# Two top-k chains in turn on VectorE, and one pool of float32 buffers for x, the result and the MLP's activations

## The chip, the cores and the metric

The kernel runs on one core of one Trainium2 chip. The metric is the device time of one execution in microseconds. The kernel before was run three times: 1166.22, 1166.27 and 1168.5 us, median 1166.27. A profiler recorded one more execution; its rows are shown further below.

## The reference

The inputs are q, k and v of shape 4 x 8 x 576 x 64 (batch, heads, sequence, head size, float32) and the weights of two MLPs, each 512 x 2048 and 2048 x 512, which come as float64. The output is 2304 x 512 float32.

```python
scores = scale * np.matmul(q, k.transpose(0, 1, 3, 2))          # 576 x 576 for each of 32 heads
kth = np.partition(scores, -32, axis=-1)[..., -32:-31]
scores = np.where(scores >= kth, scores, -1e9)                  # the 32 largest of each row stay
attn = softmax(scores); x = attn @ v                            # 2304 tokens x 512 (heads side by side)
h = np.maximum(x @ w_in, 0.0);  x = h * h @ w_out               # first MLP
h = x @ w2_in;  x = (h * np.clip(h + 3, 0, 6) / 6) @ w2_out     # second MLP
```

## The kernel before, in words

**Numbers.** Every matrix is scaled by a power of two and split into two float16 parts, a high and a low one; a product is three float16 matmuls (high x high, high x low, low x high). The float64 weights are turned to float32 by integer operations on VectorE (lines 363 and 366), completed by an addition on GpSimd (line 413), bounded by a Gram matmul (line 429) and split through TensorE and ScalarE (lines 537 to 546), for the last matrix through ScalarE and GpSimd.

**Attention.** The 576 query rows of a batch are four blocks of 128 and one of 64; a block has a tile for each head, in the block of 64 rows one for each pair of heads. That makes 20 blocks and 144 tiles. A tile goes through these steps, each a task on one engine (function `attend`):

- TensorE multiplies q and k into PSUM (`qk`, line 768); ScalarE evacuates the scores to a float32 buffer S (line 774). There are three S buffers.
- VectorE finds the 32 largest of each row in seven large steps: the eight largest of S (line 782); then three times: replace the eight found (line 787, from S into W the first time, later W in place) and take the eight largest of W (line 790). In the kernel before there is one W buffer.
- VectorE scales the 32nd largest (line 799, "the threshold"), ScalarE makes a Relu of the distance to it (line 804, tile E), GpSimd subtracts that from S (line 807, "the mask"; it frees S), ScalarE takes the exponential (line 812).
- ScalarE and GpSimd split the result (lines 818 and 822), a DMA transposes it, TensorE multiplies by v (line 841).

**Between attention and MLP.** For each block `x_operand` copies the normalised product from PSUM to the float32 tile x (line 913), takes its norm (lines 922 and 926), scales x in place (line 933), and splits it (line 936 on ScalarE, line 939 on GpSimd). Then x is free.

**The MLPs.** The two blocks of 64 rows of neighbouring batches are joined, so there are 18 units of 128 rows. Each MLP is four groups per unit, 144 groups in all: 48 up-projection matmuls (line 1083) into one of two PSUM banks h, on ScalarE a Relu into a float32 tile r (line 1090 in the first MLP, line 1092 in the second), a square on ScalarE (line 1095) or a gate on VectorE (line 1098), the split (line 1105 on ScalarE, line 1108 on GpSimd; it frees r), and 12 output matmuls (line 1115) into `acc`. A unit's result is scaled from PSUM into the float32 tile o on ScalarE (line 1187) and stored by a DMA.

**What sets the order.** All steps are tasks of a planner that runs while the program is built. It simulates the five engines with given costs; whenever an engine is free it takes, of the tasks whose inputs and buffers are there, the one with the lowest key, offset + slope x position from the table `PRIO`. A buffer pool is a list of free slots, taken at a task's start and given back when the last user is done. The planner writes out one fixed order for each engine, and on the chip each engine works through its own in that order, waiting on semaphores. In the kernel before, pool `f` has two buffers and serves r alone; pool `x` has one and serves x and o.

Of the kernel before, what the change touches and what calls it, by code (L numbers as in the profile page):

```python
# [9 lines left out]
F32 = mybir.dt.float32  # L10
# [9 lines left out]
P = 128  # L20
# [12 lines left out]
class Plan:  # L33
# [7 lines left out]
    def pool(self, **sizes):  # L41
        for name, n in sizes.items():
            self.pools[name] = list(range(n))
# [21 lines left out]
    def free(self, name, owner, *users):  # L65
        e = [len(users), name, owner]
        for u in users:
            u.rel.append(e)
# [66 lines left out]
def tile_topk_attention_moe_moe2(  # L135
# [12 lines left out]
    B, H, S, D = q.shape  # L148
# [37 lines left out]
    task, free = plan.task, plan.free  # L186
    size, ncol = {}, [0]

    def pool(name, n, shape, dtype, where=None):

        plan.pool(**{name: n})
        size[name] = (shape, dtype, where or sb)
# [7 lines left out]
    def take(name, label=None):  # L200
        if name == "stg":
            return stg[plan.current.slot[name]]
        if isinstance(size[name], int):
            c = size[name] + plan.current.slot.get(name, 0)
            return scalars[:, c:c + 1]
        shape, dtype, where = size[name]
        return where.tile(shape, dtype, tag=f"{name}{plan.current.slot[name]}", name=label or name, bufs=1)
# [5 lines left out]
    acc_t = ps.tile([P, 2, 512], F32, name="acc")  # L213
    plan.pool(acc0=1, acc1=1)
    pool("S", SBUFS, [P, S], F32)
    pool("W", 1, [P, S], F32)
    pool("E", 2, [P, S], F32)
    pool("wc", 2, [P, 2 * S], F16)
    pool("wT", WTB, [P, 2 * S // P, P], F16)
# [3 lines left out]
    pool("vv", 4, [P, 2, 2, NCH, D], F16)  # L223
    plan.pool(stg=2)
    pool("qf", 1, [P, 4, D], F32)
    pool("x", XBUFS, [P, H, D], F32)
    pool("f", FBUFS, [P, 512], F32)
    pool("hl", HBUFS, [P, 2, KD, P], F16)
    pool("ghl", GBUFS, [P, 2, 512], F16)
# [653 lines left out]
    def x_operand(i):  # L883
# [3 lines left out]
        u = unit[i]  # L887
        o = off[i]
        tail = j == NFULL
        ntl = NHP if tail else H  # L890
        box = {}
# [11 lines left out]
                                        op0=ALU.mult, op1=ALU.mult)  # L903

        def copy():
            box["x"] = x = take("x")
            if o == 0:
                T["hl", u] = take("hl")
            a_ = T["av", i]
            for t in range(ntl):  # L910
                for hh in range(2 if tail else 1):
                    rows = slice(hh * TAIL, hh * TAIL + TAIL) if tail else slice(0, P)
                    nc.scalar.activation(x[0:n, 2 * t + hh if tail else t, :], a_[rows, t * D:(t + 1) * D], AF.Copy,  # L913
                                         scale=box["rv"][rows, t:t + 1])
# [26 lines left out]
        def flip():  # L941
# [4 lines left out]
        t1 = task("DVE", 0.3, ("xinv", first[i]), inverse, deps=masks, alloc=["rv"])  # L946
        free("sums", masks[0], t1)
        t2 = task("POOL", 1.0, ("xscales", first[i]), scales, deps=[t1] + [vv_task[b, hp][1] for hp in range(NHP)])
        avs = [av_tasks[i, t] for t in range(ntl)]
        t3 = task("ACT", 1.6, ("xcopy", first[i]), copy, deps=[t2, *avs, hl_task.get(u)],  # L950
                  alloc=["x"] + (["hl"] if o == 0 else []))
        hl_task.setdefault(u, t3)
        free("rv", t1, t3)
        free("av", avs[0], t3)
# [6 lines left out]
        t8 = task("ACT", act(H * D) + 0.09, ("xevac", first[i]), scaled, deps=[t7])  # L961
        t9 = task("ACT", act(H * D), ("xhigh", first[i]), high, deps=[t8])
        t10 = task("POOL", gps(H * D), ("xlow", first[i]), low, deps=[t9])
        free("x", t3, t10)
        l_ = task("SP", 1.25, ("xflip", first[i]), flip, deps=[t10], lat=WLAT)
        free("xh", t5, l_)
        opd_task.setdefault((0, u), []).append(l_)
# [88 lines left out]
    pos = {}  # L1056
# [5 lines left out]
    acc_task, ca_task, up_tasks = {}, {}, {}  # L1062
# [110 lines left out]
    def second_layer(u):  # L1173
        n = usize[u]
        for g in range(KF // (4 if n == P else 2)):
            group(1, u, g)
        free("hl", hl_task[u], up_tasks[1, u])
        box = {}

        def scale():  # L1180
            box["oc"] = take("oc")
            nc.gpsimd.tensor_scalar(box["oc"], T["ca", u], wp["c4"][:, 0:1], 1.0, op0=ALU.mult, op1=ALU.mult)

        def evac(ch):
            rows = min(P, n - ch * P)
            box["o", ch] = take("x", "o").rearrange("p h d -> p (h d)")
            nc.scalar.activation(box["o", ch][0:rows], acc_t[0:rows, 1 if n == P else ch, :], AF.Copy,
                                 scale=box["oc"][0:rows])

        def store(ch):  # L1190
            for i in units[u]:
                if off[i] // P == ch:
                    b, j = order[i]
                    r0, o_ = b * S + j * P, off[i] - ch * P
                    nc.sync.dma_start(out[r0:r0 + nof[i], :], box["o", ch][o_:o_ + nof[i]])

        t1 = task("POOL", 0.25, ("oscale", pos[1, u, 0]), scale, deps=[ca_task[u], wchain[3]], alloc=["oc"])
        free("ca", ca_task[u], t1, up_tasks[1, u])
        evacs = []
        for ch in range(-(-n // P)):  # L1200
            t2 = task("ACT", 0.57, ("oevac", pos[1, u, 0]), lambda ch=ch: evac(ch), deps=[t1, acc_task[1, u, ch]], alloc=["x"])
            free("acc1" if n == P else f"acc{ch}", acc_task["first", 1, u], t2)
            t4 = task("SP", 0.7, ("store", pos[1, u, 0]), lambda ch=ch: store(ch), deps=[t2])
            free("x", t2, t4)
            evacs.append(t2)
        free("oc", t1, *evacs)

# [45 lines left out]
def first_of(order, b):  # L1253
# [8 lines left out]
XBUFS = 1  # L1262
# [18 lines left out]


PRIO = {
    "load0": (340.23, 0.014),
    "load1": (350.41, 0.164),
    "load2": (928.87, 0.102),
    "load3": (-360.56, 0.044),
    "conv0": (67.49, 0.032),
    "bits0": (-334.56, 0.363),
    "add0": (363.46, 0.095),  # L1290
    "gram0": (733.07, 0.252),
    "conv1": (-463.48, 6.177),
    "bits1": (-2000.78, 3.588),
    "add1": (755.49, 12.573),
    "gram1": (-359.57, 3.788),
    "conv2": (-82.75, 2.263),
    "bits2": (-74.87, 5.088),
    "add2": (-377.68, 0.472),
    "gram2": (-991.89, 0.269),
    "conv3": (-1.27, 0.102),  # L1300
    "bits3": (-226.43, 28.692),
    "add3": (-84.33, 84.284),
    "gram3": (-161.59, 0.926),
    "norm": (219.01, 13.853),
    "high0": (-1412.47, 0.238),
    "low0": (-24.71, 0.477),
    "scaled0": (120.91, 11.399),
    "rest0": (-103.76, 1.596),
    "high1": (14.57, 0.624),
    "low1": (127.85, 0.860),  # L1310
    "scaled1": (330.42, 0.525),
    "rest1": (-81.15, 22.480),
    "high2": (293.37, 0.024),
    "low2": (630.00, 0.444),
    "scaled2": (806.32, 3.448),
    "rest2": (215.58, 5.372),
    "high3": (626.80, 1.338),
    "low3": (626.39, 0.081),
    "scaled3": (-343.44, 0.430),
    "rest3": (697.07, 8.977),  # L1320
    "qsquare": (632.65, 7.129),
    "qtotal": (-1166.11, 0.296),
    "qscale": (-195.35, 1.307),
    "ksquare": (141.52, 0.440),
    "ktotal": (-181.14, 0.255),
    "kscale": (-641.06, 0.456),
    "vsquare": (-1289.92, 1.322),
    "vtotal": (-247.36, 0.604),
    "vscale": (-270.58, 0.132),
    "clear": (-377.61, 0.641),  # L1330
    "kload": (52.44, 1.333),
    "vload": (216.40, 1.003),
    "qload": (178.65, 0.151),
    "qhigh": (232.24, 1.506),
    "qlow": (352.49, 0.502),
    "khigh": (1105.20, 0.462),
    "klow": (-595.14, 0.742),
    "vhigh": (649.09, 0.140),
    "vlow": (296.69, 1.624),
    "kflip": (-92.81, 0.020),  # L1340
    "qscales": (-1577.85, 0.028),
    "qflip": (-1853.07, 8.317),
    "qk": (-107.90, 1.290),
    "evac": (-234.65, 0.662),
    "topk": (301.64, 0.948),
    "bias": (-1723.17, 0.048),
    "lowest": (299.95, 1.000),
    "below": (164.49, 1.525),
    "mask": (-161.55, 1.964),
    "expo": (58.25, 1.189),  # L1350
    "whigh": (667.72, 2.141),
    "wlow": (812.95, 0.224),
    "wflip": (-102.44, 0.805),
    "av": (609.90, 0.441),
    "xinv": (-211.49, 3.990),
    "xscales": (-221.33, 3.583),
    "xcopy": (-212.46, 0.097),
    "xflip": (335.99, 3.918),
    "xsquare": (23.27, 0.207),
    "xtotal": (-357.75, 0.055),  # L1360
    "xscale": (184.03, 11.039),
    "xevac": (-411.77, 1.057),
    "xhigh": (-2455.71, 0.319),
    "xlow": (355.78, 0.352),
    "common": (420.79, 5.138),
    "ysquare": (2109.22, 0.583),
    "ytotal": (-237.40, 1.777),
    "yflip": (-429.37, 0.932),
    "yscale": (262.86, 0.157),
    "yhigh": (-121.73, 0.079),  # L1370
    "ylow": (174.25, 0.109),
    "whole": (-351.50, 4.507),
    "up0": (668.30, 0.933),
    "up1": (894.69, 0.154),
    "relu0": (1086.57, 27.916),
    "relu1": (279.33, 0.149),
    "gsquare": (4638.92, 0.182),
    "gate": (248.94, 0.591),
    "ghigh0": (3795.54, 8.302),
    "ghigh1": (325.99, 6.612),  # L1380
    "glow0": (2397.49, 17.389),
    "glow1": (2070.02, 0.416),
    "acc0": (350.93, 0.363),
    "acc1": (718.32, 1.415),
    "oscale": (372.67, 0.013),
    "oevac": (-2257.15, 0.248),
    "store": (268.89, 1.259),
}

_INS = ["q", "k", "v", "moe_w_in", "moe_w_out", "moe2_w_in", "moe2_w_out"]  # L1390
# [25 lines left out]
```

## Time and profile before

| what | value |
|---|---|
| median of three runs | 1166.27 us |
| profiled execution | 1168.76 us |
| its span | 1167.0 us |
| mean granted TensorE clock | 0.98 of full |
| busy: TensorE, VectorE, ScalarE, GpSimd | 1037.1, 981.5, 926.9, 835.5 us |
| HBM read, written | 48.23 MB, 4.72 MB |

The span runs from the first to the last recorded instruction. A busy time is the sum over an engine's instructions with overlaps counted once. Three stages can be told apart: the weights' preparation beside the first attention tiles, then attention and MLP side by side, then MLP alone.

### The profile page before, as it was taken

The numbers are of one execution on the slowest core, as the hardware profiler recorded it, in microseconds if no ns is written. First come the engines' busy times: TensorE is split into PE (matmuls) and PEld (weight loads), VectorE is DVE, ScalarE is ACT, GpSimd is POOL, SyncE is SP. The second block draws the span as 40 slices with busy tenths as digits, with TensorE's granted clock in tenths as the row PEclk, the third lists the DMA queues.
The fourth block names the chain that finished last, engine by engine and source line by source line (L and its number), as shares of the span: only waits on it lengthen the run. The fifth ranks groups of instructions, "written<-read, shape, count | busy, mean of one in ns | idle before, by whom it ended". The sixth has DMA issues, their size and how long they took to land.

```text
span 1167.0 us, 31626 instructions
## 1 busy us (share of the span) xinstructions
PE 1037.1 (89%) x12076; PEld 743.5 (64%) x12076; DVE 981.5 (84%) x2299; ACT 926.9 (79%) x1888; POOL 835.5 (72%) x1112
## 2 busy tenths in 40 slices
PE   2375679778998999999999999999999999999998
PEld 1232346455776676776768777776767677777765
DVE  5899799999985899999999999999889999994111
ACT  7668798889996888888988779888978778886432
POOL 5878788489975776878768788777676777876221
PEclk9998699998999999999999999999999999999999
DMA  8978666523675444366564454445843433434000
GB/s 214 259 252 249 221 170 133 110 54 57 107 119 124 74 80 73 75 93 108 99 130 86 83 84 77 86 75 94 137 80 65 84 77 62 79 70 71 19 20 19
DMA packets 314824, 121.60 MB, mean 104 GB/s; under 512 B 295600, under 2 KB 303792, under 8 KB 314672
## 3 DMA queue, kind: packets, MB, share of 16 engines
q1 hardware_dynamic: 314672, 119.58, 49.4%
q8 instruction: 94, 1.54, 0.6%
q14 instruction: 58, 0.48, 0.1%
HBM read 48.23 MB, written 4.72 MB: 45 GB/s over the span
## 4 chain that ended last, share of the span: by engine, by line
PE 37%; DVE 21%; ACT 17%; POOL 10%; issue 6%; DMA 6%; SPq 2%; POOLq 0%; ACTq 0%; DVEq 0%
PE acc L1115 16%; PE hb L1083 14%; DVE W L787 6%; DVE m L790 5%; POOL E L807 3%; PE sp L768 2%; ACT E L812 2%; DVE cv L363 2%; PE av L841 2%; DVE m L782 2%; ACT S L774 2%; DVE w L366 2%; DMA w<-in_moe_w_in_dram 1%; ACT x L913 1%; DMA kT<-kn 1%
## 5 line engine op out<-in xcount | busy, mean ns | idle before, releaser
L1115 PE MATMUL acc<-w,ghl 128*128 128x512 f16 x1728 | 451.8, 382 | 15.5 <-POOL ghl L1108 4.9
L1083 PEld LDWEIGHTS <-w 128*128 128x128 f16 x6912 | 415.8, 98 | 75.7 <-issue 6.1
L1083 PE MATMUL hb<-hl,w 128*128 128x128 f16 x6912 | 453.3, 219 | 4.7 <-DVE r L1098 2.1
L790 DVE MAX8 m<-W 128x8 f32<-128x576 f32 x432 | 326.2, 755 | 6.1
L1108 POOL TENSOR_TENSOR ghl<-r,ghl 128x512 f16<-128x512 f32 x144 | 168.2, 1171 | 109.0 <-ACT ghl L1105 104.0
L807 POOL TENSOR_TENSOR E<-S,E 128x576 f32<-128x576 f32 x144 | 203.8, 1415 | 48.1 <-ACT E L804 47.9
L1115 PEld LDWEIGHTS <-ghl 128*128 128x128 f16 x1728 | 153.6, 99 | 130.4 <-issue 19.1
L787 DVE MATCH_REPLACE8 W<-m,W 128x576 f32<-128x576 f32 x288 | 213.9, 743 | 0.0
L822 POOL TENSOR_TENSOR wc<-E,wc 128x512 f16<-128x512 f32 x144 | 167.0, 1160 | 36.5 <-ACT wc L818 35.8
L774 ACT ACTIVATE S<-sp 128x576 f32<-128x576 f32 x144 | 93.3, 648 | 48.0 <-POOL E L807 44.1
L812 ACT ACTIVATE E<-E,scalars,scl 128x576 f32<-128x576 f32 x144 | 124.4, 864 | 1.8 <-POOL E L807 1.7
L804 ACT ACTIVATE E<-S,scalars 128x576 f32<-128x576 f32 x144 | 111.5, 774 | 12.3 <-DVE scalars L799 10.9
L782 DVE MAX8 m<-S 128x8 f32<-128x576 f32 x144 | 108.1, 751 | 15.0 <-ACT S L774 13.6
L768 PE MATMUL sp<-kT,qT 128*128 128x288 f16 (+1 forms) x640 | 98.8, 295 | 21.0 <-ACT S L774 13.8
L1105 ACT ACTIVATE ghl<-r 128x512 f16<-128x512 f32 x144 | 90.0, 628 | 25.6 <-DVE r L1098 16.9
L787 DVE MATCH_REPLACE8 W<-m,S 128x576 f32<-128x576 f32 x144 | 106.9, 743 | 0.0
L1098 DVE SCALAR_TENSOR_TENSOR r<-r,hb 128x512 f32<-128x512 f32 x72 | 49.0, 680 | 64.6 <-ACT r L1092 63.7
L818 ACT ACTIVATE wc<-E 128x576 f16<-128x576 f32 x144 | 97.8, 680 | 0.6
L841 PEld LDWEIGHTS <-wT 128*128 128x128 f16 (+1 forms) x2240 | 84.0, 102 | 21.7 <-issue 5.8
L768 PEld LDWEIGHTS <-qT 128*128 128x128 f16 (+1 forms) x640 | 56.0, 103 | 54.9 <-issue 28.7
L841 PE MATMUL av<-vv,wT 128*128 128x64 f16 (+1 forms) x2240 | 90.9, 196 | 0.0
L794 POOL TENSOR_SCALAR scalars<-m,scl 128x1 f32<-128x1 f32 x144 | 39.5, 274 | 69.9 <-ACT E L812 27.7
(125 smaller groups left out, 1306.4 us busy)
## 6 DMA issues: line engine op xcount, KB each, us to landing
w<-in_moe_w_in_dram SPq DMA_DIRECT2D x32, 512.0 KB, 5.5
w<-in_moe_w_out_dram SPq DMA_DIRECT2D x29, 512.0 KB, 4.5
out_dram<-o SPq DMA_DIRECT2D x16, 256.0 KB, 2.3
qf<-in_q_dram SPq DMA_DIRECT2D x31, 128.0 KB, 2.8
stg<-in_k_dram SPq DMA_DIRECT2D x12, 256.0 KB, 3.2
stg<-in_v_dram SPq DMA_DIRECT2D x12, 256.0 KB, 3.1
wT<-wc SPq DMA_TRANSPOSE x144, 3.3
stg<-in_moe_w_out_dram SPq DMA_DIRECT2D x6, 256.0 KB, 4.3
```

The source lines that it names most:

```text
L768: nc.tensor.matmul(dst, qT[:, 2 * ((2 * hp + hh) % 4) + a, 0:M], kflat[:, hh * SPAD + c * HALF:hh * SPAD + (c + 1) * HALF], start=a == 0, ...
L774: nc.scalar.activation(T["S", s].rearrange("p (c n) -> p c n", c=2), T["sp", s][:, :, 0:HALF], AF.Copy)
L782: nc.vector.max(m[:, 0:8], T["S", s])
L787: nc.vector.match_replace(out=T["W", s], in_to_replace=m[:, 8 * c - 8:8 * c], in_values=T["S", s] if c == 1 else T["W", s], imm_value=-3.0e38)
L790: nc.vector.max(m[:, 4 * r:4 * r + 8], T["W", s])
L807: nc.gpsimd.tensor_tensor(T["E", s], T["S", s], T["E", s], op=ALU.subtract)
L812: nc.scalar.activation(T["E", s], T["E", s], AF.Exp, bias=T["nb", s], scale=T["scl", ("q", i, half)][:, hp % 2:hp % 2 + 1], accum_out=T["s ...
L822: nc.gpsimd.tensor_tensor(wc[:, S + TAIL:], e[:, 0:S - TAIL], wc[:, 0:S - TAIL], op=ALU.subtract)
L841: nc.tensor.matmul(out_[cols, t * D:(t + 1) * D], wT[0:kr, a, cols], vv[0:kr, vb, hh, c, :], start=n_ == 0, stop=n_ == len(prods) - 1)
L1083: nc.tensor.matmul(box["h"][:, fi * n:(fi + 1) * n], wt[2 * m][:, kk * 4 + f // 4, a, f % 4 * P:(f % 4 + 1) * P], hl[:, c, kk, 0:n], start ...
L1108: nc.gpsimd.tensor_tensor(flat(box["g"][:, 1]), flat(box["r"]), flat(box["g"][:, 0]), op=ALU.subtract)
L1115: nc.tensor.matmul(o_, gl[d], wt[2 * m + 1][:, f, a, :], start=f == 0 and (a, d) == (0, 0), stop=f == KF - 1 and (a, d) == PRODS[-1])
```

## The change

The pool W gets a second buffer, the pool x is dropped and its two users take from `f`, and the whole table PRIO has other numbers. Nothing else differs; the code behind line 226 moves up by one line, so that line 787 of the kernel before is line 786 now.

```diff
@@ pools
-    pool("W", 1, [P, S], F32)
+    pool("W", 2, [P, S], F32)
...
-    pool("x", XBUFS, [P, H, D], F32)
     pool("f", FBUFS, [P, 512], F32)
@@ x_operand
-            box["x"] = x = take("x")
+            box["x"] = x = take("f", "x").rearrange("p (h d) -> p h d", h=H)
...
-                  alloc=["x"] + (["hl"] if o == 0 else []))
+                  alloc=["f"] + (["hl"] if o == 0 else []))
...
-        free("x", t3, t10)
+        free("f", t3, t10)
@@ second_layer
-            box["o", ch] = take("x", "o").rearrange("p h d -> p (h d)")
+            box["o", ch] = take("f", "o")
...
-            t2 = task("ACT", 0.57, ("oevac", pos[1, u, 0]), lambda ch=ch: evac(ch), deps=[t1, acc_task[1, u, ch]], alloc=["x"])
+            t2 = task("ACT", 0.57, ("oevac", pos[1, u, 0]), lambda ch=ch: evac(ch), deps=[t1, acc_task[1, u, ch]], alloc=["f"])
...
-            free("x", t2, t4)
+            free("f", t2, t4)
@@ PRIO (every row differs)
-    "topk": (301.64, 0.948),
+    "topk": (881.41, 157.552),
```

VectorE's order in the middle of the attention, before (m and W carry a number for each tile):

```order
L787 MATCH_REPLACE W_11041<-m_10933,S_10918 128x576
L799 TENSOR_SCALAR scalars_83<-m_10824 128x1
L790 MAX m_10933<-W_11041 128x8
L782 MAX m_11070<-S_11060 128x8
L787 MATCH_REPLACE W_11041<-m_10933,W_11041 128x576
L790 MAX m_10933<-W_11041 128x8
L787 MATCH_REPLACE W_11041<-m_10933,W_11041 128x576
L790 MAX m_10933<-W_11041 128x8
L782 MAX m_11136<-S_11120 128x8
L787 MATCH_REPLACE W_11150<-m_11070,S_11060 128x576
L799 TENSOR_SCALAR scalars_83<-m_10933 128x1
```

The same engine at a like place in the changed order:

```order
L781 MAX m_10962<-S_10934 128x8
L789 MAX m_10879<-W_10948 128x8
L786 MATCH_REPLACE W_10977<-m_10962,S_10934 128x576
L786 MATCH_REPLACE W_10948<-m_10879,W_10948 128x576
L789 MAX m_10962<-W_10977 128x8
L789 MAX m_10879<-W_10948 128x8
L786 MATCH_REPLACE W_10977<-m_10962,W_10977 128x576
L786 MATCH_REPLACE W_10948<-m_10879,W_10948 128x576
L789 MAX m_10962<-W_10977 128x8
L789 MAX m_10879<-W_10948 128x8
L786 MATCH_REPLACE W_10977<-m_10962,W_10977 128x576
L798 TENSOR_SCALAR scalars_83<-m_10879 128x1
```

Before, the tile 10933 runs its steps one behind the other, and a first maximum of one or two later tiles stands in between; now the steps of tiles 10962 and 10879 take turns, each on its own W.

ScalarE's order around one copy of x late in the attention, before (x is held from line 913 to a GpSimd instruction behind line 936; r is taken by lines 1090 and 1092):

```order
L913 ACTIVATE x_15371<-av_15463,rv_15135 128x64 x8
L274 ACTIVATE xh_15258<-acc_90,scalars_83 64x512 x2
L1092 ACTIVATE r_15427<-hb_15278,bias3_80,scalars_83 128x512
L1105 ACTIVATE ghl_15461<-r_15427 128x512
L804 ACTIVATE E_15483<-S_15096,scalars_83 128x576
L774 ACTIVATE S_15521<-sp_15336 128x576
L812 ACTIVATE E_15483,sums_15219<-E_15483,scalars_83,scl_14215 128x576
L1092 ACTIVATE r_15535<-hb_15429,bias3_80,scalars_83 128x512
L922 ACTIVATE xh_15541,scalars_83<-x_15371 128x512
```

And around a copy of x at a like place of the changed order:

```order
L912 ACTIVATE x_16205<-av_15376,rv_15950 128x64 x8
L817 ACTIVATE wc_16239<-E_16072 128x576
L921 ACTIVATE xh_16255,scalars_83<-x_16205 128x512
L1091 ACTIVATE r_16263<-hb_16146,bias3_80,scalars_83 128x512
L803 ACTIVATE E_16281<-S_16060,scalars_83 128x576
L817 ACTIVATE wc_16288<-E_16135 128x576
L932 ACTIVATE x_16205<-x_16205,scalars_83 128x512
L1104 ACTIVATE ghl_16328<-r_16263 128x512
L935 ACTIVATE xh_16255<-x_16205 128x512
```

Before, two Relus stand between the copy of x and its norm, and there are buffers for both beside x; now one Relu stands between the copy and the last pass over x, and x and that r hold both buffers of `f`.

## Rows read from the trace of the kernel before

In rows 1 the five engine columns are TensorE's matmuls, its weight loads, VectorE, ScalarE and GpSimd; behind them stand the granted TensorE clock, the DMA share and GB/s.

**Rows 1.** Busy time by stage: us, then each engine's busy us (instructions).

```profile
0.00:171.00 171.00, 91.73 (x538) 50.74 (x539) 143.39 (x320) 130.95 (x254) 129.17 (x153) 0.91 0.79 228
171.00:280.00 109.00, 89.06 (x931) 59.66 (x929) 103.97 (x244) 96.89 (x202) 84.70 (x112) 0.94 0.46 93
280.00:1083.00 803.00, 776.99 (x9754) 577.08 (x9753) 723.66 (x1712) 669.98 (x1387) 602.61 (x831) 1.00 0.49 88
1083.00:1167.00 84.00, 79.36 (x858) 56.03 (x856) 10.47 (x25) 29.04 (x49) 18.97 (x18) 1.00 0.08 20
sum 1167.00, PE 1037.15 PEld 743.51 DVE 981.49 ACT 926.86 POOL 835.45; mean PE 259.29 PEld 185.88 DVE 245.37 ACT 231.72 POOL 208.86
```

**Rows 2.** TensorE in order of time: first MLP matmul, last attention product.

```profile
171.23 0.83 PE L1083 MATMUL hb<-hl,w 128*128 128x128 f16 x12
...
1081.09 0.57 PE L841 MATMUL av<-vv,wT 128*128 128x64 f16 x14
```

**Rows 3.** TensorE's waits up to 171 us: us, times, longest.

```profile
PE acc L429 <- POOL w L413: 31.7, 19, 6.0
```

**Rows 4.** TensorE's waits from 171 to 280 us.

```profile
PE sp L768 <- ACT S L774: 7.3, 6, 2.2
```

**Rows 5.** TensorE's waits from 280 us to the end.

```profile
PE acc L1115 <- ACT o L1187: 4.0, 7, 1.6
...
PE sp L768 <- ACT S L774: 2.7, 6, 0.8
PE hb L1083 <- DVE r L1098: 2.1, 4, 0.7
PE acc L1115 <- DVE xh L278: 2.0, 5, 1.0
```

**Rows 6.** VectorE in order of time: start us, us, instruction.

```profile
629.19 0.74 DVE L790 MAX8 m<-W 128x8 f32<-128x576 f32 x1
629.85 0.74 DVE L782 MAX8 m<-S 128x8 f32<-128x576 f32 x1
...
632.22 0.74 DVE L787 MATCH_REPLACE8 W<-m,W 128x576 f32<-128x576 f32 x1
633.00 0.76 DVE L790 MAX8 m<-W 128x8 f32<-128x576 f32 x1
```

**Rows 7.** Groups of instructions: busy us, mean ns, idle time before and its releaser.

```profile
L807 POOL TENSOR_TENSOR E<-S,E 128x576 f32<-128x576 f32 x144 | 203.8, 1415 | 48.1 <-ACT E L804 47.9
...
L774 ACT ACTIVATE S<-sp 128x576 f32<-128x576 f32 x144 | 93.3, 648 | 48.0 <-POOL E L807 44.1
...
L804 ACT ACTIVATE E<-S,scalars 128x576 f32<-128x576 f32 x144 | 111.5, 774 | 12.3 <-DVE scalars L799 10.9
```

**Rows 8.** Who waited for whom over the whole span.

```profile
ACT r L1092 <- PE hb L1083: 32.4, 23, 4.3
...
DVE m L782 <- ACT S L774: 13.6, 22, 3.5
```

**Rows 9.** ScalarE and GpSimd in order of time: one hold of x.

```profile
608.88 1.72 ACT L913 ACTIVATE x<-av,rv 128x64 f32<-128x64 f32 x8
...
615.13 1.16 POOL L939 TENSOR_TENSOR xh<-x,xh 128x512 f16<-128x512 f32 x1 [0.31 <-ACT xh L936]
```

**Rows 10.** DMA issues: count, KB each, us to landing.

```profile
out_dram<-o SPq DMA_DIRECT2D x16, 256.0 KB, 2.3
```

**Rows 11.** ScalarE and GpSimd in order of time: one hold of r.

```profile
560.83 0.76 ACT L1092 ACTIVATE r<-hb,bias,scalars 128x512 f32<-128x512 f32 x1
...
564.21 1.16 POOL L1108 TENSOR_TENSOR ghl<-r,ghl 128x512 f16<-128x512 f32 x1
```

**Rows 12.** TensorE in order of time in the tail.

```profile
1100.07 2.84 PE L1083 MATMUL hb<-hl,w 128*128 128x128 f16 x48
1102.75 0.81 PE L1115 MATMUL acc<-w,ghl 128*128 128x512 f16 x3
1103.40 0.83 PE L1083 MATMUL hb<-hl,w 128*128 128x128 f16 x12
```

More of the change, by code (lines that the diff above doesn't have):

```diff
@@ L1283 @@
 PRIO = {
[L1284 to L1344, printed above, removed]
-    "topk": (301.64, 0.948),
-    "bias": (-1723.17, 0.048),
-    "lowest": (299.95, 1.000),
@@ L1348 @@
[L1348 to L1387, printed above, removed]
+    "load0": (330.64, 0.027),
+    "load1": (424.53, 0.219),
+    "load2": (474.37, 0.400),
+    "load3": (205.78, 0.035),
+    "conv0": (-108.19, 0.003),
+    "bits0": (585.78, 11.459),
+    "add0": (-16.78, 0.116),
+    "gram0": (-466.88, 26.451),
@@ new lines @@
+    "conv1": (-62.87, 28.786),
+    "bits1": (-200.42, 1.670),
+    "add1": (-1832.14, 68.662),
+    "gram1": (892.62, 11.683),
+    "conv2": (-1824.09, 4.284),
+    "bits2": (386.21, 1.471),
+    "add2": (120.44, 0.016),
+    "gram2": (-104.76, 0.124),
+    "conv3": (83.13, 2.971),
+    "bits3": (349.57, 1.183),
+    "add3": (-816.12, 2.440),
+    "gram3": (367.88, 0.192),
+    "norm": (291.38, 0.716),
+    "high0": (-422.34, 0.431),
+    "low0": (-153.53, 16.248),
+    "scaled0": (878.09, 0.291),
@@ new lines @@
+    "rest0": (-179.62, 17.317),
+    "high1": (-281.29, 8.368),
+    "low1": (-1177.47, 1.995),
+    "scaled1": (1413.61, 0.068),
+    "rest1": (-2109.59, 110.077),
+    "high2": (-838.01, 0.002),
+    "low2": (-335.30, 0.133),
+    "scaled2": (-136.70, 10.956),
+    "rest2": (-1157.12, 42.079),
+    "high3": (469.79, 0.020),
+    "low3": (298.62, 0.021),
+    "scaled3": (338.35, 0.057),
+    "rest3": (-110.68, 753.241),
+    "qsquare": (-1807.18, 3.491),
+    "qtotal": (-666.13, 0.599),
+    "qscale": (-14.84, 0.045),
@@ new lines @@
+    "ksquare": (269.97, 0.437),
+    "ktotal": (77.06, 0.590),
+    "kscale": (375.83, 1.069),
+    "vsquare": (79.33, 0.196),
+    "vtotal": (-500.99, 1.186),
+    "vscale": (44.64, 0.486),
+    "clear": (165.16, 3.256),
+    "kload": (-2399.15, 1.313),
+    "vload": (-129.79, 1.366),
+    "qload": (-133.20, 0.033),
+    "qhigh": (-78.69, 4.398),
+    "qlow": (-2002.61, 0.043),
+    "khigh": (-501.68, 2.646),
+    "klow": (-2021.34, 0.125),
+    "vhigh": (641.29, 0.112),
+    "vlow": (306.95, 2.046),
@@ new lines @@
+    "kflip": (256.85, 0.039),
+    "qscales": (-449.24, 0.010),
+    "qflip": (-1978.70, 2.965),
+    "qk": (-1301.96, 10.269),
+    "evac": (347.80, 4.524),
+    "topk": (881.41, 157.552),
+    "bias": (876.68, 0.109),
+    "lowest": (-59.86, 1.347),
+    "below": (119.67, 1.004),
+    "mask": (-975.30, 0.031),
+    "expo": (558.34, 2.941),
+    "whigh": (238.85, 7.052),
+    "wlow": (992.85, 0.139),
+    "wflip": (-124.52, 0.072),
+    "av": (389.64, 0.511),
+    "xinv": (-54.21, 0.294),
+    "xscales": (-1669.36, 3.445),
@@ new lines @@
+    "xcopy": (-13.01, 1.365),
+    "xflip": (111.69, 0.306),
+    "xsquare": (177.21, 0.022),
+    "xtotal": (102.36, 0.674),
+    "xscale": (-176.99, 15.209),
+    "xevac": (-42.21, 0.225),
+    "xhigh": (-1871.87, 0.023),
+    "xlow": (-1105.31, 0.101),
+    "common": (-1039.84, 4.887),
+    "ysquare": (333.79, 0.255),
+    "ytotal": (-86.38, 0.333),
+    "yflip": (1147.81, 0.085),
+    "yscale": (-1800.69, 0.012),
+    "yhigh": (-834.08, 0.530),
+    "ylow": (-412.19, 0.016),
+    "whole": (453.35, 14.321),
@@ L1388 @@
+    "up0": (392.67, 0.570),
+    "up1": (4118.58, 0.156),
+    "relu0": (287.31, 39.542),
+    "relu1": (317.87, 0.375),
+    "gsquare": (246.60, 0.019),
+    "gate": (-216.97, 0.675),
+    "ghigh0": (-47.91, 50.626),
+    "ghigh1": (-103.95, 4.694),
+    "glow0": (-998.67, 28.483),
+    "glow1": (276.42, 1.022),
+    "acc0": (1131.15, 0.003),
+    "acc1": (1190.03, 4.334),
+    "oscale": (541.86, 0.001),
+    "oevac": (884.31, 0.374),
+    "store": (-1707.71, 0.117),
 }
```

## The prediction

> **What bounds the kernel now.** I read busy time by stage first, then TensorE's waits in each stage, and last VectorE instruction by instruction. Over the span two engines are near full [rows 1]: TensorE 1037.15 of 1167 us, VectorE 981.49. The stages tell them apart. Up to 171 us, when the first MLP matmul starts [rows 2], TensorE is busy for 91.7 us and idle for 79.3; from 171 to 280 it is idle for 19.9; from 280 to 1083, where attention and MLP run together, for 26.0 of 803; behind 1083, just after the last attention product [rows 2], for 4.6, and its granted clock is full in the last two stages. So behind 280 us this is a TensorE kernel with VectorE close beside it (723.7 of 803 us busy), and all that a change can win from TensorE's idle time is 129.9 us. The first 79.3 belong to the loading and converting of the weights; their largest wait is that for GpSimd's add to a converted slab [rows 3]. The tail of 84 us holds MLP work alone and is full.
>
> **The change, part by part.**
>
> *The alternation.* A tile's chain on VectorE is a maximum on S, then three times a replacement and a maximum on W. Neighbours that hang on each other and neighbours that don't are both in the trace [rows 6]. The maximum at 629.19 is independent of its successor at 629.85: 0.66 us from start to start. The replacement at 632.22 wrote what the maximum at 633.00 reads: 0.78. A dependent neighbour costs 0.12 us. Counted over the order of all 144 tiles, 332 of the replacements and maxima stand directly behind the instruction that wrote what they read; in the changed order 56 do. 276 x 0.12 = 33 us of VectorE's time go. Ten of the 332 stand in the first 12 tiles, 16 in the next 12 and 48 in the 12 behind these, so most of it falls behind 280 us.
>
> [...]
>
> *The life of a score buffer.* There are three S buffers; tile k's scores can be evacuated when the mask of tile k-3 is done. Behind the threshold that loop is the Relu, the mask and the evacuation, 0.77 + 1.41 + 0.65 = 2.83 us of work on two engines [rows 7], and four hand-overs. In the order before, VectorE has between the threshold of tile k-3 and the first maximum of tile k a median of 5 large instructions, some 5 x 0.72 = 3.6 us (the mean of the two distances); in the changed order 8, some 8 x 0.66 = 5.3 us. The edge is thin now and the trace shows it: ScalarE waits 44.1 us in front of evacuations for the mask [rows 7], VectorE 13.6 us for the evacuation [rows 8], TensorE 7.3 us between 171 and 280 and 2.7 behind [rows 4, 5]. With two chains open rather than three these waits should largely go. What is late next is TensorE itself: ScalarE's Relu of the second layer alone waits 32.4 us for the up-projection [rows 8].
>
> *What of it reaches the end.* Only TensorE's idle time can be won, so the terms come from there. Up to 171 us: 10 dependent neighbours are 1.2 us; the first up-projection has 192 Gram matmuls ahead of it in TensorE's order where it had 212, and of the 31.7 us of their wait [rows 3] 20/212 are 3.0. Bounds 0 and -4.2; I take -3, close to the far end, because both come before the first MLP matmul can start. From 171 to 280: the 7.3 us of TensorE's wait for S [rows 4]; bounds 0 and -7.3, I take -4. From 280 on: the waits that end with VectorE or with S are 2.7 + 2.1 + 2.0 = 6.8 us [rows 5]; bounds 0 and -6.8, I take -5. The rest there is untouched.
>
> *The shared float32 buffers.* Before, x and o have one buffer between them and the MLP's r two. In the changed kernel x, o and r draw on the same two. x is held from its copy to GpSimd's subtraction, 608.88 to 616.29 us = 7.4 [rows 9], for 20 blocks 148 us; o is held through its store, 2.3 us to landing [rows 10], with its evacuation about 3 us x 18 = 54. In that time one buffer is left for r. An r is held from its Relu to GpSimd's subtraction, 560.83 to 565.37 = 4.5 us [rows 11]. The 144 groups of the MLP spread over 1167 - 171 = 996 us, one in 6.9 us, so one buffer does on the average; in the tail TensorE works through a group in 2.68 + 4 x 0.65 = 5.3 us [rows 12], and one does there too, by less. What does not fit is two Relus close together inside a hold, which the order before has. The changed order sets at most one Relu between x's copy and its last ScalarE pass, where before there were up to three. A wait, if any, stands in front of a Relu, of x's copy or of o's evacuation on ScalarE; behind it in that queue stand Exp and the evacuation of the next scores, for which VectorE would wait. Two product banks let TensorE run one group (2.68 us of up-projection) ahead, which covers part of the 4.5. Lower bound 0; below that nothing speaks, since a buffer less frees no engine. Upper bound 38 holds x (4.5 - 2.68) = 69 us. I take +1, close to 0, because the mean distance of groups exceeds the hold.
>
> *The rest.* TensorE's instructions are the same in number and kind; W's second buffer costs only memory.
>
> Sum: -3 - 4 - 5 + 1 = -11. The profiled execution took 1168.76 us (span 1167.0 and 1.76 around it), so it would become 1157.8; the median of the runs before, 1166.27, lies 2.5 below the profiled one and becomes 1155.3. I predict 1155; the likeliest case's own range is 1146 to 1162.
>
> **The rivals.**
>
> *TensorE takes nothing (no change).* For it: TensorE is 97% busy in the main stage [rows 1], and the waits that I count there are many small ones. Against: the 44.1 us of waits in the S loop hold up a ScalarE queue that also feeds the MLP. VectorE's 33 us would become idle time of VectorE: 1166, within 2.3 us. [...]
>
> *More than forecast.* If the attention's chain on VectorE sets the pace of TensorE too, all 33 us come through: 1166 - 33 = 1133. For it: VectorE is 88% busy up to 280 us and 90% in the main stage, and behind the last attention product the changed order leaves 108 up-projection and 24 output matmuls more than before, 108 x 0.056 + 24 x 0.217 = 11 us of TensorE's work [rows 12], so attention is set to end that much work sooner. Against: in the main stage TensorE has only 26 us to give, and part of the 99 before it is bound by loads. 1133 is the far end and 1140 the middle.
>
> *Slower: the float32 buffers decide.* Place: in front of the MLP's Relu, x's copy and o's evacuation on ScalarE, while the other f buffer is held. Price: if each of the 38 holds delays TensorE by 0.6 us (a third of the 1.8 in the bound), 38 x 0.6 = 23 us against the 12 gained, 1177. It decides from 12 / 38 = 0.32 us a hold. For it: where up to three Relus stood inside an x hold they must now stand elsewhere, and o's evacuation, for which TensorE already waits 4.0 us in 7 places [rows 5], needs a buffer that an r or x may hold, with TensorE's next second-layer accumulation behind it. Against: 6.9 us per group, 4.5 per hold.
>
> **How the numbers follow.** Forecast 0.50, more than forecast 0.15, no change 0.14, slower 0.21. A difference under 0.2% (2.3 us) can't be told from none here. Faster by more than that takes the first two, 0.65; same 0.14; slower 0.21. The range leaves out about a tenth at each end: the far part of the larger gain, below 1136, and the half of the slower case above 1175.
>
> **What would show it.** In the changed kernel's trace, independent neighbours 0.66 us apart should be the rule on VectorE and its busy time fall by 20 to 33 us; ScalarE's wait for the mask in front of evacuations should drop from 44.1 to under 15. TensorE's idle time should be near 76, 16 and 21 us in the same three stages, and the last attention product end near 1060 rather than 1082, with some 95 us behind it. It is wrong if Relu, x's copy and o's evacuation together wait more than 15 us for GpSimd's subtraction or a store, or if TensorE's idle time in the main stage exceeds 30.

## The result, and the profile after

The changed kernel takes 1150.64 us (median of 4 runs, 1150.15 to 1152.52) against 1167.3 for the kernel before on the same chip: a ratio of 0.9858, 95% interval [0.9844, 0.9872], 16.6 us faster. The forecast was 1155, and the likeliest case's own range 1146 to 1162. The profiled execution's span fell from 1167.0 to 1148.3 us.

Busy time by stage in the changed kernel, with the columns of [rows 1]; the third border is again just behind the last attention product:

```profile
0.00:171.00 171.00, 94.42 (x642) 56.96 (x643) 144.09 (x323) 130.25 (x252) 129.86 (x152) 0.91 0.78 228
171.00:280.00 109.00, 89.69 (x849) 57.25 (x847) 101.82 (x248) 99.25 (x208) 86.80 (x116) 0.92 0.47 97
280.00:1053.00 773.00, 758.28 (x9604) 567.43 (x9602) 688.56 (x1703) 661.80 (x1375) 595.74 (x826) 1.00 0.51 91
1053.00:1148.30 95.30, 91.10 (x991) 64.55 (x988) 12.08 (x28) 32.75 (x58) 21.32 (x20) 0.99 0.10 21
sum 1148.30, PE 1033.51 PEld 746.20 DVE 946.54 ACT 924.05 POOL 833.72; mean PE 258.38 PEld 186.55 DVE 236.64 ACT 231.01 POOL 208.43
```

TensorE's idle time in the four stages is 171 - 94.4 = 76.6, then 19.3, 14.7 and 4.2 us, where [rows 1] gave 79.3, 19.9, 26.0 and 4.6. So of the 18.7 us of the span 15.1 are idle time, 11.3 of these in the main stage, and 3.6 are TensorE's busy time. VectorE is busy for 34.9 us less. The Gram matmuls' wait for GpSimd up to 171 us, and the wait for scores from 171 to 280, are nearly what they were in [rows 3] and [rows 4]:

```profile
PE acc L428 <- POOL w L412: 30.9, 15, 6.4
```

```profile
PE sp L767 <- ACT S L773: 6.8, 7, 3.3
```

The two marks of [rows 2] in the changed kernel, TensorE in order of time:

```profile
157.78 0.83 PE L1082 MATMUL hb<-hl,w 128*128 128x128 f16 x12
...
1051.63 0.57 PE L840 MATMUL av<-vv,wT 128*128 128x64 f16 x14
```

The MLP starts 13.4 us earlier and the attention ends 29.5 us earlier; the tail behind it is 96 us long where it was 85.

VectorE in order of time, as [rows 6]:

```profile
574.71 0.75 DVE L781 MAX8 m<-S 128x8 f32<-128x576 f32 x1
575.38 0.74 DVE L789 MAX8 m<-W 128x8 f32<-128x576 f32 x1
576.04 0.07 DVE L786 MATCH_VALUE_LOAD W<-m,S 128x8 f32 x1
576.10 0.74 DVE L786 MATCH_REPLACE8 W<-m,S 128x576 f32<-128x576 f32 x1
576.76 0.14 DVE L798 TENSOR_SCALAR scalars<-m 128x1 f32<-128x1 f32 x1
```

Behind a large instruction that the next one does not hang on, the next starts 0.66 us later, 575.38 to 576.04 and 576.10 to 576.76, as between independent ones before.

Who waited for whom over the whole span: us in total, times, longest. These answer to [rows 7, 8]; the Relu's, x's and o's waits for GpSimd and for the store are those for a buffer of `f`:

```profile
ACT r L1091 <- PE hb L1082: 45.1, 27, 4.6
...
ACT S L773 <- POOL E L806: 26.7, 30, 2.6
...
DVE m L781 <- ACT S L773: 12.0, 12, 2.6
...
ACT r L1089 <- POOL ghl L1107: 4.7, 5, 1.7
...
ACT o L1186 <- POOL ghl L1107: 1.4, 2, 0.7
ACT x L912 <- DMA out_dram<-o: 1.2, 1, 1.2
...
ACT r L1091 <- POOL ghl L1107: 0.3, 1, 0.3
...
ACT r L1091 <- DMA out_dram<-o: 0.2, 1, 0.2
```

The wait for the mask fell from 44.1 to 26.7, that for a float32 buffer is 7.8 us in all, and the second layer's Relu waits longer for TensorE than before, 45.1 against 32.4.

TensorE's waits from 280 us to the end, as [rows 5]:

```profile
PE acc L1114 <- ACT xh L995: 2.8, 6, 1.0
PE acc L1114 <- DVE xh L277: 2.5, 6, 1.3
PE sp L767 <- ACT S L773: 1.9, 6, 0.7
PE acc L1114 <- ACT o L1186: 1.9, 6, 0.8
...
PE sp L767 <- DMA kT<-kn: 0.7, 1, 0.7
```

Of the kernel before, the row for the transposed K, which [rows 5] leaves out:

```profile
PE sp L768 <- DMA kT<-kn: 3.6, 4, 1.6
```

One view that I had not built on shows a difference: the chain of waits that ended last, by engine, first of the kernel before, then of the changed one.

```profile
PE 37%; DVE 21%; ACT 17%; POOL 10%; issue 6%; DMA 6%; SPq 2%; POOLq 0%; ACTq 0%; DVEq 0%
```

```profile
PE 56%; ACT 19%; DVE 10%; POOL 6%; issue 5%; DMA 2%; SPq 2%; ACTq 0%; POOLq 0%; DVEq 0%
```

Before, the chain passes through all engines, TensorE in little over a third of it; now it runs through TensorE for more than half.

### The profile page after: what moved, and what is told of

Its sections match the earlier page's. It is cut to its first block, busy times and chain, and to the rows that moved or that the text cites. A ratio compares the mean times of both kernels' runs of the same rounds, so it can differ in the third digit from the quotient of the medians.

```text
span 1148.3 us, 31513 instructions
## 1 busy us (share of the span) xinstructions
PE 1033.5 (90%) x12076; PEld 746.2 (65%) x12076; DVE 946.5 (82%) x2299; ACT 924.0 (80%) x1888; POOL 833.7 (73%) x1112
## 4 chain that ended last, share of the span: by engine, by line
PE 56%; ACT 19%; DVE 10%; POOL 6%; issue 5%; DMA 2%; SPq 2%; ACTq 0%; POOLq 0%; DVEq 0%
PE acc L1114 24%; PE hb L1082 22%; PE sp L767 4%; PE av L840 3%; DVE W L786 2%; DVE m L789 2%; POOL E L806 2%; ACT S L773 2%; ACT E L811 2%; ACT E L803 1%; ACT x L912 1%; ACT w L545 1%; DVE cv L362 1%; ACT w L539 1%; ACT r L1091 1%
## 5 line engine op out<-in xcount | busy, mean ns | idle before, releaser
L1114 PE MATMUL acc<-w,ghl 128*128 128x512 f16 x1728 | 444.3, 381 | 10.5 <-ACT xh L995 2.8
L789 DVE MAX8 m<-W 128x8 f32<-128x576 f32 x432 | 315.1, 749 | 0.9
L773 ACT ACTIVATE S<-sp 128x576 f32<-128x576 f32 x144 | 93.3, 648 | 30.3 <-POOL E L806 26.7
L1091 ACT ACTIVATE r<-hb,bias,scalars 128x512 f32<-128x512 f32 x72 | 56.0, 778 | 46.7 <-PE hb L1082 45.1
L767 PEld LDWEIGHTS <-qT 128*128 128x128 f16 (+1 forms) x640 | 55.7, 103 | 52.4 <-issue 26.7
```

The lines of the kernel that those rows point to most:

```text
L767: nc.tensor.matmul(dst, qT[:, 2 * ((2 * hp + hh) % 4) + a, 0:M], kflat[:, hh * SPAD + c * HALF:hh * SPAD + (c + 1) * HALF], start=a == 0, ...
L773: nc.scalar.activation(T["S", s].rearrange("p (c n) -> p c n", c=2), T["sp", s][:, :, 0:HALF], AF.Copy)
L789: nc.vector.max(m[:, 4 * r:4 * r + 8], T["W", s])
L1114: nc.tensor.matmul(o_, gl[d], wt[2 * m + 1][:, f, a, :], start=f == 0 and (a, d) == (0, 0), stop=f == KF - 1 and (a, d) == PRODS[-1])
```

## The experiments

Theory A: VectorE's saved time is what was won, in whatever order. Theory B: the planner's new order won it. C, D and F give a part to the score buffers' loop (the S loop: Relu, mask and evacuation), E to TensorE and VectorE together. Except in two runs every kernel keeps the order of the one it is made from: the planner's costs are unchanged, and only what a task emits differs. Ratios are to the kernel before on the same chip, and the us lost or won are worked out from them; the changed kernel itself is at 0.9858. Busy times, waits and chains are those of the one profiled execution.

**VectorE's time put back into the changed kernel.**

```diff
                 nc.vector.max(m[:, 4 * r:4 * r + 8], T["W", s])
+                if r == 2:
+                    nc.vector.max(m[:, 24:32], T["W", s][:, 0:160])
```

> The changed kernel in its own order, with one more MAX8 per tile on VectorE over 160 columns of W (its result is overwritten); about 0.23 us x 144 = 33 us, what the alternation saves. Theory A, VectorE's saved time is what was won: 12 to 20 us slower than the changed kernel (1163 to 1171). Theory B, the order won it (attention ahead of the MLP in TensorE's order, thresholds spread wider), whatever VectorE's time: under 5 us slower (below 1156).

Measured: 1164.36 us, 0.9959 [0.9939, 0.998], so 0.0101 or 11.8 us of the gain are lost for 28.3 us more of VectorE's busy time (974.8). The chain turns to VectorE:

```profile
DVE 38%; PE 28%; ACT 16%; POOL 7%; issue 5%; DMA 3%; SPq 2%; ACTq 0%; POOLq 0%; DVEq 0%
```

As theory A says, for this order. The change took 34.9 us of busy time from VectorE and this run put 28.3 back, so the 5 us that are left of the gain are the most that the order is worth without VectorE's shorter chains.

**GpSimd's time added in front of the mask, changed kernel.**

```diff
         def mask():
+            nc.gpsimd.tensor_scalar(scalars[:, size["dm"]:size["dm"] + 1], bias3, 1.0, 1.0, op0=ALU.mult, op1=ALU.mult)
```

> The changed kernel in its own order, with one more small GpSimd instruction (128x1, some 0.27 us x 144 = 39 us) in front of each mask, which lengthens the loop that frees a score buffer. Theory A: GpSimd has slack, 0 to 4 us slower. Theory C, the score-buffer loop's latency is what was won: 8 us or more slower (above 1158).

Measured: 1158.67 us, 0.9924 [0.9902, 0.9946], 7.7 us lost for 23.7 us of GpSimd's busy time, between the two theories' numbers and close to C's. GpSimd is 73% busy in the changed kernel, and still a third of the added time is felt. ScalarE waits longer for the mask, where the changed kernel has 26.7:

```profile
ACT S L774 <- POOL E L808: 33.1, 40, 2.8
```

That points to the loop that frees a score buffer; that no other work of GpSimd, which comes later too, cost the time isn't shown.

**VectorE's time taken out of the kernel before.**

```diff
-                nc.vector.max(m[:, 4 * r:4 * r + 8], T["W", s])
+                nc.vector.max(m[:, 4 * r:4 * r + 8], T["W", s][:, 0:356] if r == 2 else T["W", s])
```

> The kernel before in its own order, with the second of the four maxima of each tile taken over 356 of 576 columns (the result is then another): 0.23 us x 144 = 33 us less on VectorE, no dependence changed. Theory A: 12 to 20 us faster than before (1147 to 1155). Theory B: within 5 us of before (1161 to 1167).

Measured: 1167.02 us, 0.9989 [0.9978, 0.9999], 1.3 us for 26.8 us of VectorE's busy time. Theory A falls in the old order. VectorE waits longer for the evacuation, 23.5 us where [rows 8] has 13.6, and ScalarE as long as before for the mask:

```profile
ACT S L774 <- POOL E L807: 44.3, 51, 2.7
...
DVE m L782 <- ACT S L774: 23.5, 39, 3.4
```

**The old table with the new buffers.** The change without its PRIO hunk; here the planner makes another order.

> Two W buffers and the shared float32 buffers with the numbers of the old table PRIO: the planner's order then has 128 dependent neighbours (332 before, 56 in the changed kernel) and a median of 8 large instructions between a threshold and the third next first maximum, as the changed one. Theory A: 204 x 0.12 = 24 us of VectorE's time won, so most of the gain, 1153 to 1159. Theory B, the table's own order won it: no gain or a loss, 1163 and above.

Measured: 1240.4 us, 1.0617 [1.0594, 1.064]. Theory B. This order has 128 dependent neighbours and the wide spacing of thresholds, and loses 72 us nevertheless, with its largest TensorE wait behind 280 us in front of score products:

```profile
PE sp L767 <- ACT S L773: 24.5, 18, 4.8
PE acc L1114 <- POOL ghl L1107: 9.2, 4, 5.3
```

Its last attention product starts at 1115.6 us, 34 later than before. What in it goes wrong first I did not take apart. Part of the loss may be the clock: the granted clock is 0.958 in the profiled execution (0.98 before), and TensorE is busy 1060.6 us instead of 1037.1 with the same matmuls. The run says that fewer dependent neighbours do not make up for what this order and the shared buffers lose. The opposite, the new table with one W buffer, leaves the planner without a task that it can start, so it can't be run.

**VectorE's time added to the kernel before** (the first diff, on the kernel before).

> The kernel before in its own order with the same extra MAX8 per tile (33 us more on VectorE). Since 33 us less bought it 1 us, theory D says that its order has VectorE waiting for scores anyway (S loop and TensorE set the pace) and only part of the added time is felt: under 8 us slower (below 1176). Theory A (VectorE's time is the price in either order): 12 to 20 us slower (1180 to 1188).

Measured: 1176.72 us, 1.0081 [1.0064, 1.0098], 9.5 us for 27.8 more. Between the two theories' numbers. The old order is on a kink: more VectorE time costs a third of itself, less brings next to nothing.

**TensorE's time taken out of the kernel before.**

```diff
                 kk, (a, c) = n_ // 3, PRODS[n_ % 3]
+                if n_ == 5:
+                    continue
```

> The kernel before in its own order with one of the twelve up-projection matmuls of each 128 columns left out (576 of 6912; the result is then another): 576 x 0.0557 = 32 us less on TensorE. If TensorE's work sets the end, 24 to 32 us faster (1136 to 1144); if attention on VectorE and the S loop set it up to 1082 us and only the tail behind is TensorE's, only the tail's share, 55 of 576 matmuls or 3 us, and at most 10 us faster.

Measured: 1166.65 us, 0.9988 [0.9974, 1.0002], 1.4 us, with an interval that includes no gain, for 25.8 us less of TensorE's busy time. The granted clock may hide a part: eight of the ten executions had 0.974 to 0.976 and took 1165.4 to 1169.6 us, the other two, the profiled one among them, had 0.982 and 0.978 and took 1162.7 and 1162.2; the kernel before had 0.978 to 0.982. Even these two win some 5 us, not 24. TensorE's work by itself did not set the end of the kernel before, though it was 97% busy in the main stage; the chain then runs through it for less than a quarter:

```profile
DVE 26%; PE 23%; ACT 22%; POOL 14%; issue 8%; DMA 6%; SPq 2%; POOLq 0%; ACTq 0%; DVEq 0%
```

**Both taken out of the kernel before** (the two diffs together).

> The kernel before in its own order, with both reductions at once: 33 us less on VectorE and one of twelve up-projection matmuls left out (32 us less on TensorE). Each alone gave 1 us. Theory E: two chains of nearly equal length end together, one through TensorE's MLP work and one through VectorE's attention work, so that both have to be shorter: 12 to 25 us faster than before (1143 to 1155). Theory F: a third one, the S loop through ScalarE and GpSimd, is as long: under 6 us faster (above 1161).

Measured: 1163.72 us, 0.9967 [0.9953, 0.9981], 3.9 us, at a granted clock of 0.974 to 0.979 where the kernel before had 0.977 to 0.982. VectorE has 29.4 us less and TensorE 21.3, and the end moves by a few us: theory F. The wait for the mask is 47.0 us here.

**The mask shortened, kernel before.**

```diff
-            nc.gpsimd.tensor_tensor(T["E", s], T["S", s], T["E", s], op=ALU.subtract)
+            nc.gpsimd.tensor_tensor(T["E", s][:, 0:456], T["S", s][:, 0:456], T["E", s][:, 0:456], op=ALU.subtract)
-FAR = 2.0 ** 96
+FAR = 1.0
```

> The kernel before in its own order with the mask on GpSimd over 456 of 576 columns alone (33 us less on GpSimd, a shorter S loop; threshold's factor 1; the result is then another), VectorE's work whole. With VectorE's 33 us as well it was 8 us faster, with VectorE's alone 1. If the S loop through ScalarE and GpSimd is the limit of the order before: 5 to 9 us faster (1158 to 1162). If VectorE's chain and the S loop limit it together: under 3 us (above 1164).

Measured: 1160.01 us, 0.9939 [0.9922, 0.9955], 7.1 us for 37.0 us less of GpSimd's busy time. The wait for the mask falls to near what it is in the changed kernel, with VectorE's work whole:

```profile
ACT r L1092 <- PE hb L1083: 34.0, 24, 4.3
...
ACT S L774 <- POOL E L807: 29.9, 39, 2.4
```

Two things make the 7.1 us an upper bound for the loop. In the profiles the first MLP matmul starts at 168.3 us instead of 171.2, so 2.9 of the 9.0 us between the spans are won where GpSimd also converts weights, and the rest by the end of the attention. And the granted clock is 0.984 in all four executions, against 0.978 to 0.982 of the kernel before: over the 49 executions of the kernel before on four chips 0.001 of clock goes with some 0.4 us, so by my estimate up to 2 us are the clock's.

**The mask and VectorE together, kernel before.**

> The kernel before in its own order with 33 us less on VectorE (second maximum over 356 columns) and the mask on GpSimd over 456 of 576 columns (0.23 us x 144 = 33 us less on GpSimd, and a shorter S loop; the threshold's factor is 1 instead of 2^96, so that what is left unmasked stays finite; the result is then another). If the S loop took up what VectorE saved (theory D), the two together give 8 us or more (below 1160). If TensorE's order is what holds it, again under 4 us (above 1164).

Measured: 1159.19 us, 0.993 [0.9915, 0.9944], 8.2 us: 1 us more than the mask alone, which is inside both intervals. Of the three, the mask was the one that the old order felt by itself, though it was also cut by more, 37 us against 26. What part of it is the S loop's length and what part GpSimd's time, the cut mask can't tell, since it shortens both; a fourth S buffer in the old order, which would tell, was not run.

**VectorE's time taken out of the changed kernel** (the third diff).

> The changed kernel in its own order with 33 us less on VectorE (second maximum over 356 columns; the result is then another). Adding 33 us cost 14. If VectorE still sets the pace, 8 us or more faster (below 1143); if TensorE is what is left (idle 15 us in its main stage), under 4 us (above 1146).

Measured: 1150.75 us, 0.9861 [0.9843, 0.9879]: nothing, for 26.9 us less of VectorE's busy time.

**TensorE's time taken out of the changed kernel.**

> The changed kernel in its own order with the same matmul of each twelve left out (32 us less on TensorE). Less VectorE work gave it nothing, and its chain of waits runs to 56% through TensorE. Theory E: TensorE is now the longer of the two chains and VectorE has room: 12 us or more faster (below 1139). If the two are balanced again as before: under 5 us (above 1146).

Measured: 1137.87 us, 0.9746 [0.972, 0.9772], 13.1 us for 27.8 us less. Where the kernel before gave 1.4, the changed one gives half of what is taken. The chain then turns to VectorE again, which may be what keeps the other half:

```profile
DVE 30%; PE 28%; ACT 21%; POOL 7%; issue 6%; DMA 5%; SPq 2%; ACTq 0%; POOLq 0%; DVEq 0%
```

**The shared buffers alone** (the change without W's second buffer and without the new table; another order).

> The kernel before with one W buffer and the old table, but x and o taken from the pool f: the price of the shared buffers without the alternation. The order has 347 dependent neighbours (332 before). My sum has +1 us for the sharing: within 4 us of before (1163 to 1171). The rival of the slower side had 0.6 us for each of 38 holds: 20 us or more slower (above 1187).

Measured: 1193.29 us, 1.022 [1.0189, 1.0251], 25.7 us slower: near the number of the slower rival. ScalarE waits for a buffer of `f` in front of the Relus and x:

```profile
ACT r L1089 <- POOL ghl L1107: 4.5, 5, 1.8
ACT x L912 <- POOL ghl L1107: 4.3, 4, 2.2
...
ACT x L912 <- DMA out_dram<-o: 1.5, 1, 1.5
...
ACT r L1091 <- POOL ghl L1107: 1.1, 2, 0.5
```

These are 11.4 us, not much more than the 7.8 in the changed kernel, so the rival's mechanism is not shown to be the cause. The order, which the planner had to lay around the buffers, differs too: its last attention product starts at 1097.2 us, 16 later than before, and 732 up-projection matmuls stand behind it instead of 660. And TensorE is busy 8.8 us longer for the same matmuls, at a granted clock of 0.973 in the profiled execution. How the 25.7 us divide among these stays open.

## Why the prediction was right, and where its steps were not

**The alternation** did to VectorE what was forecast: 33 us by the count of neighbours, 34.9 measured, with the spacing of 0.66 us. The count is no better than some 6 us, though: it gives 24 us less for the old table with the new buffers, where VectorE is busy 18.3 us less, and 2 us more for the shared buffers alone, where it is 6.3 more. The distances from start to start tell the two kinds of neighbour apart, 0.66 us for the independent and 0.78 for the dependent ones in [rows 6].

**The life of a score buffer** was a right mechanism, under-weighed. I had it as the reason for a few waits of TensorE, 4 us of the sum between 171 and 280 and a share of 5 behind. In the runs the mask, its GpSimd step, is what the old order felt most: a shorter one brings 7.1 us, of which the granted clock and the time before the MLP have a part, VectorE's 26.8 us alone 1.3, TensorE's 25.8 alone 1.4. The wait for the mask fell to 26.7, not under 15: ScalarE still comes to it early 30 times.

**TensorE as the bound** was wrong for the kernel before. The step "behind 280 us this is a TensorE kernel" took a busy share of 97% for the limit, and 25.8 us less of it moved the end by 1.4, by some 5 in the two executions with the clock of the kernel before. It holds better for the changed kernel (13.1 for 27.8). That the idle time of TensorE is the pool from which gains come did hold as bookkeeping: 15.1 of 18.7 us.

**The terms by stage.** The time came inside the range partly by luck: the total was near, but most of it did not come from the waits that the sum was built on. Up to 171 us -3 was forecast and -2.7 measured, yet the term's reason failed: the Gram matmuls' wait for GpSimd, which was to lose 3.0 us, went from 31.7 to 30.9. The idle time fell as the first MLP matmul starts 13.4 us earlier, which puts 104 matmuls more into that stage; what lets it start earlier was not tested. Between 171 and 280 -4 was forecast and -0.6 measured; TensorE's wait for scores there is 6.8 us where [rows 4] has 7.3. From 280 on -5 was forecast, with +1 for the shared buffers, and -11.7 measured, 11.3 of it in the main stage. The three waits behind the -5, 6.8 us together, fell by 2.4: that for S from 2.7 to 1.9, that for line 1098 from 2.1 to none, that for line 278 rose from 2.0 to 2.5. The failed step is "the rest there is untouched": some 9 us came from that rest, among it the wait for o's evacuation, from 4.0 to 1.9, and that for the transposed K, from 3.6 to 0.7. TensorE's busy time, -3.6, was put at nothing in the sum, and no run shows why it fell. The attention ended at 1052 us, 8 before the forecast 1060; the tail, 96 against 95, came out as the counts of matmuls behind it said.

**The shared buffers.** +1 was right for the changed order, in the sense that its waits for a buffer are 7.8 us on ScalarE, under the 15 set as a limit, against 2.5 + 1.6 + 0.6 = 4.7 before:

```profile
ACT r L1092 <- POOL ghl L1108: 2.5, 1, 2.5
...
ACT r L1090 <- POOL ghl L1108: 1.6, 3, 1.0
...
ACT x L913 <- DMA out_dram<-o: 0.6, 2, 0.5
```

As a price of the sharing it was far off: with the old table it costs 25.7 us. The slower rival's number came out there; its price per hold is not shown. That the sharing costs little here goes with the new table: the same buffers cost 25.7 us, and with a second W 72 us, in the orders that the old table gives.

**What the gain is, then.** Not one of its parts: with 28.3 of VectorE's 34.9 us put back, the new order keeps 0.0041 of 0.0142 (about 5 us); VectorE's saved time in the old order gives 0.0011; the new buffers without the table lose. Shown is that neither VectorE's nor TensorE's time by itself held the old order, that a shorter mask helped it, that TensorE's work counts in the new one, and that the new one loses when VectorE's time is put back or the mask comes later. That the S loop, rather than GpSimd's time, was the old order's limit is argued, not shown. Which of the table's many moves closed TensorE's small waits in the main stage stays open.

## What to carry to other kernels

Before counting an engine's saved time as gain, read who waits for whom around the buffer loop that feeds it, and ask for the share of each engine in the chain of waits. A share spread over four engines is a warning that less work on the busiest one may hardly move the end (1.4 us here). It does not say which reduction will: GpSimd had 10% of the chain before, and its shorter mask brought the most. In a program with a fixed order for each engine, what an instruction is worth depends on the order: 27 to 28 us of VectorE, taken or added, were worth 0, 1, 9 or 12 us here. Freed memory or a shared buffer has a price only together with the schedule that is laid around it, so measure it with the schedule, and also apart.

## What the runs showed of the hardware

A MAX8 over 160 columns is recorded with 0.31 us, and its successor, which does not depend on it, starts 0.23 us behind it; for the MAX8 over 576 columns at 575.38 us of the changed kernel, further above, the two numbers are 0.74 and 0.66. In both the recorded duration is 0.08 us longer than the distance to the next start. VectorE in order of time in the changed kernel with the extra maximum:

```profile
602.33 0.31 DVE L791 MAX8 m<-W 128x8 f32<-128x160 f32 x1
602.56 0.74 DVE L789 MAX8 m<-W 128x8 f32<-128x576 f32 x1
```

I had not expected that an instruction over 128x1 on GpSimd, adding 23.7 us of busy time in all or 0.16 us each, would cost the kernel 7.7 us as one more instruction for each tile.
